# SwiGLU feed-forward on one core: the first weight slabs doubled, their queue changed, and both x tiles transposed before the first matmul

## The chip, the core and the metric

The kernel runs on one core of a Trainium2 chip. The metric is device time in microseconds (us) of one execution; the time before is the median of 3 runs. One more execution was taken by the profiler.

## The reference

```python
B, S, D, F = 1, 2048, 512, 1376     # x (B,S,D), w_gate and w_up (D,F), w_down (F,D), all bf16
def reference(x, w_gate, w_up, w_down):
    g = silu(x @ w_gate)
    u = x @ w_up
    return (g * u) @ w_down
```

## The kernel before

All instructions are written out by hand for five engines: SP (SyncE) and ACT (ScalarE) issue the loads, PE (TensorE) multiplies, ACT applies silu, DVE (VectorE) multiplies gate by up, and both ACT and DVE copy results out of PSUM. Semaphores order them.

**Tiles.** The hidden width F is cut into 10 full tiles of 128 and a rest of 96, the 2048 tokens into 4 chunks of 512, and the contraction over D into 4 steps (`dk`). The first stage makes, chunk by chunk, one gate group and one up group for each F tile: 4 matmuls of 128x128 weights with 512 tokens, into one of 8 PSUM banks in turn. ACT and DVE turn a pair of groups into a tile of `hT_sb`. The rest of 96 is packed into further groups: one for each chunk on PE (`X`, 4 matmuls of 512 tokens as well) and one for each two chunks (`Y`). The second stage multiplies by `w_down`, in strips of 32 rows, and stores 16 token tiles.

**x.** The matmuls need x with D on the partitions (`xT_sb`). For the first 256 tokens two tiles of 128 tokens are loaded as they are (`xn_sb`, `load_xn`, L113) and transposed on PE against an identity (`transposes`, L362), 4 transposes a tile, each into a bank of its own (banks 0 to 3 for tile 0, 4 to 7 for tile 1). DVE copies the even steps and ACT the odd ones into `xT_sb` (L300 and L288). `xt_ready[i, dk]` holds which engine makes the copy of tile i and step dk, and its place. All other tokens come through a transposing DMA (`load_x`, L93), tokens 256 to 383 and 384 to 511 in one each.

**Weights.** Gate and up weights come in slabs of F tiles (L104): tile 0, tile 1, tiles 2 and 3, tiles 4 to 6, the rest. One slab of one tile is 128 KB, read in runs of 256 B (128 columns of bf16); one of two tiles is 256 KB in runs of 512 B. ACT issues gate slab 0 and x tile 1 (`loads_on_scalar`, L119). SP issues x tile 0, up slab 0, the gate and up slabs of tile 1 and of tiles 2 and 3, the two transposing loads, and then all the rest (`loads_on_sync`, L123). A queue issues in order of the program and none of these loads waits for another.

**The order on PE.** PE starts with fillers on constants (`warm`, L354: 5 matmuls of 512 columns, 2 of 128). Then come the 4 transposes of x tile 0 (L371), 2 more fillers, gate tile 0 on the first 128 tokens, the transposes of x tile 1, up tile 0 on the first 128 tokens, and gate and up tile 0 on tokens 128 to 255, step by step. `first` is the list of the first 8 groups: gate and up of tiles 0 to 3 in turn. Groups 2 to 7 then run on the first 256 tokens in the order gate 1, up 1, gate 2, gate 3, up 2, up 3:

```python
for at in (2, 3, 4, 6, 5, 7):
    gu_matmuls(first[at], 0, HT)
```

After them groups 0 and 1 run on tokens 256 to 383 and 384 to 511, groups 2 to 7 on tokens 256 to 511, and from there on every group runs on 512 tokens at once. `gu_matmuls` (L347) waits for the slab that it needs, and `gu_step` (L339) in chunk 0 for the copies of the x tiles that its tokens lie in, each step for its own. A group counts as done (`s_P`) when its last token's last step is.

Of the kernel before, what the change touches and what calls it, by code (L numbers as in the profile page):

```python
# [11 lines left out]
N_GAP = 2  # L12


def bass_standalone__swiglu_ffn__prompt_kernel(nc, x, w_gate, w_up, w_down, out):
    _, S, D = x.shape
    F = w_gate.shape[1]
    P = 128
    KD = D // P
    NFF = F // P  # L20
    NFT = NFF + 1
# [7 lines left out]
    HT = SC // 2  # L29
    NXN = HT // P  # L30
    NB = 8
# [19 lines left out]
    with ExitStack() as es:  # L51
# [17 lines left out]
        banks = [bank_all[:, i, :] for i in range(NB)]  # L69
# [14 lines left out]
        def load_sem(name):  # L84
            loads[name] = sem(f"s_{name}")
            return loads[name]

        ones_w = nc.const_aps.tensor(1.0, [P, P], BF16)
        ones_m = nc.const_aps.tensor(1.0, [P, SC], BF16)
# [3 lines left out]
        def load_x(eng, name, t0, t1):  # L93
            eng.dma_start_transpose(
                xT_sb[:, :, t0:t1], xf[t0:t1, :]
            ).then_inc(load_sem(name), 16)

        def load_w(eng, name, src, base, f0, f1):
            eng.dma_start(
                w_sb[:, :, base + f0:base + f1],  # L100
                src[:, f0:f1].rearrange("(k p) f -> p k f", p=P),
            ).then_inc(load_sem(name), 16)

        slabs = [(0, 1), (1, 2), (2, 4), (4, 7), (7, NFT)]  # L104
        slab_of = {ft: a for a, b in slabs for ft in range(a, b)}

        def load_gate(eng, a, b):
            load_w(eng, f"wg{a}", w_gate, 0, a * P, min(b * P, F))

        def load_up(eng, a, b):  # L110
            load_w(eng, f"wu{a}", w_up, UPH, a * P, min(b * P, F - 32))

        def load_xn(eng, i):  # L113
            eng.dma_start(xn_sb[:, i, :], xf[i * P:(i + 1) * P, :]).then_inc(load_sem(f"xn{i}"), 16)
# [2 lines left out]
            return of[t * P:(t + 1) * P, :]  # L117

        def loads_on_scalar(act):  # L119
            load_gate(act, *slabs[0])  # L120
            load_xn(act, 1)

        def loads_on_sync(sp):  # L123
            load_xn(sp, 0)
            load_up(sp, *slabs[0])
            for a, b in slabs[1:3]:
                load_gate(sp, a, b)
                load_up(sp, a, b)
            load_x(sp, "x0b", HT, HT + P)
            load_x(sp, "x0c", HT + P, SC)  # L130
            for a, b in slabs[3:]:
                load_gate(sp, a, b)
                load_up(sp, a, b)
            load_w(sp, "wut", w_up, F - (F - 32), F - 32, F)
            for c in range(1, NSC):
                load_x(sp, f"x{c}", c * SC, (c + 1) * SC)
            sp.dma_start(
                wd_sb[:, 0:NFF, :], w_down[0:NFF * P, :].rearrange("(k p) d -> p k d", p=P)
            ).then_inc(load_sem("wd"), 16)
            load_sem("wdt")  # L140
            for y0 in (0, 64):
                sp.dma_start(wd_sb[y0:y0 + 64, T01, :], w_down[NFF * P:F - SR, :]).then_inc(loads["wdt"], 16)
            for x0 in range(0, P, SR):
                sp.dma_start(wd_sb[x0:x0 + SR, T2, :], w_down[F - SR:F, :]).then_inc(loads["wdt"], 16)
            sp.dma_start(wd_sb[0:F_LAST, TAIL, :], w_down[NFF * P:F, :]).then_inc(load_sem("wdl"), 16)
# [7 lines left out]
        def add_group(kind, **what):  # L153
            g = dict(kind=kind, at=len(groups), bank=banks[len(groups) % NB], readers=[], **what)
            groups.append(g)
            return g
# [8 lines left out]
        def tview(i, dk):  # L165
            return banks[KD * i + dk][:, 0:P // 2].bitcast(BF16)
# [46 lines left out]
        xt_ready = {}  # L213
# [19 lines left out]
        for at, t in enumerate(tiles):  # L233
# [3 lines left out]
            for c0, c1 in parts:  # L237
                g = add_group("O", t=t, c0=c0, c1=c1)
                eng = "A" if at % 2 == 1 and c0 == 0 else "D"
                op = add_op(  # L240
                    eng, g, kind="copy", out=o_sb[ob][:, c0:c1], src=g["bank"][:, 0:c1 - c0],
# [17 lines left out]
        def on_sync(sp):  # L259
            loads_on_sync(sp)  # L260
            store_tiles(sp, "S")
            for i in range(NOS):
                sp.wait_ge(s_out[i], 16 * n_store[i])
# [11 lines left out]
        def on_scalar(act):  # L275
            loads_on_scalar(act)
            act.activation(adummy[:, 0:4], zero_c, ACT.Silu)  # L277
            for op in act_ops:
                act.wait_ge(*ready(op))
                if op["kind"] == "silu":  # L280
                    if op["free"]:
                        act.wait_ge(s_D, op["free"])
                    fn = ACT.Silu
                else:
                    if op["stored"][1]:
                        act.wait_ge(*op["stored"])
                    fn = ACT.Copy
                act.activation(op["out"], op["src"], fn).then_inc(s_A, 1)  # L288
            store_tiles(act, "A")
# [13 lines left out]
        def on_tensor(pe):  # L303
            landed = set()

            def need(name, count=1):
                if name not in landed:
                    pe.wait_ge(loads[name], 16 * count)
                    landed.add(name)
# [3 lines left out]
            def after(eng, n):  # L313
                if n > read[eng]:
                    pe.wait_ge(s_A if eng == "A" else s_D, n)
                    read[eng] = n
# [6 lines left out]
            def whole(bank, dk, col, c, n0, n1):  # L323
                return pe.matmul(  # L324
                    bank[:, n0:n1], lhsT=w_sb[:, dk, col:col + P],
                    rhs=xT_sb[:, dk, c * SC + n0:c * SC + n1], start=(dk == 0), stop=(dk == KD - 1),
                )

            def gu_needs(g, n0, n1):
                c, ft = g["c"], g["ft"]  # L330
                if c > 0:
                    need(f"x{c}")
                if c == 0 and n1 > HT:
                    need("x0b")
                if c == 0 and n1 > HT + P:
                    need("x0c")
                need(("wg" if g["kind"] == "G" else "wu") + str(slab_of[ft]))

            def gu_step(g, dk, n0, n1):  # L339
                c = g["c"]  # L340
                col = (0 if g["kind"] == "G" else UPH) + g["ft"] * P
                if c == 0:
                    for i in range(n0 // P, min(n1 // P, NXN)):
                        after(*xt_ready[i, dk])
                ins = whole(g["bank"], dk, col, c, n0, n1)
                if n1 == SC and dk == KD - 1:
                    ins.then_inc(s_P, 1)  # L347

            def gu_matmuls(g, n0, n1):
                gu_needs(g, n0, n1)  # L350
                for dk in range(KD):
                    gu_step(g, dk, n0, n1)

            def warm(n, width):  # L354
                for i in range(n):
                    pe.matmul(banks[NB - 1][:, 0:width], lhsT=ones_w, rhs=ones_m[:, 0:width], start=True, stop=True)  # L356

            warm(N_WARM, SC)
            warm(N_FILL, P)
            pe.wait_ge(s_I, 1)  # L360

            def transposes(i):  # L362
                need(f"xn{i}")
                for dk in range(KD):
                    pe.matmul(  # L365
                        tview(i, dk), lhsT=xn_sb[:, i, dk * P:(dk + 1) * P], rhs=ident[:, :],
                        start=True, stop=True, is_transpose=True,
                    ).then_inc(s_X, 1)

            first = groups[0:NB]  # L370
            transposes(0)  # L371
            warm(N_GAP, P)
            gu_matmuls(first[0], 0, P)
            transposes(1)
            gu_matmuls(first[1], 0, P)
            for dk in range(KD):
                for g in first[0:2]:
                    gu_step(g, dk, P, HT)
            for at in (2, 3, 4, 6, 5, 7):
                gu_matmuls(first[at], 0, HT)  # L380
            for n0, n1 in ((HT, HT + P), (HT + P, SC)):
                for g in first[0:2]:
# [4 lines left out]
            for g in groups[NB:NO]:  # L387
# [11 lines left out]
                elif kind == "Y":  # L399
                    need(f"wu{slab_of[NFF]}")  # L400
                    for dk in range(KD):
                        for c in (2 * g["pi"], 2 * g["pi"] + 1):
# [3 lines left out]
                                rhs=xT_sb[:, dk, c * SC:(c + 1) * SC],  # L406
                                start=(dk == 0), stop=(dk == KD - 1),
# [61 lines left out]
            for g in groups[NO + TPC * (TPC - 1):]:  # L469
# [6 lines left out]
                for fk in (tailed if last else full[1:]):  # L476
                    if fk < NFF:
                        h, w = hT_sb[:, fk, t * P:(t + 1) * P], wd_sb[:, fk, c0:c1]
                    else:
# [3 lines left out]
                        stop=(fk == (NFF if last else NFF - 1)), skip_group_check=True,  # L483
# [4 lines left out]
        on_gpsimd(nc.gpsimd)  # L488
        on_scalar(nc.scalar)
        on_tensor(nc.tensor)  # L490
        on_vector(nc.vector)

# [27 lines left out]
```

## Time and profile before

| | us |
|---|---|
| time, median of 3 runs | 120.6 (120.32, 120.6, 120.76) |
| span of the profiled execution | 118.6 |
| TensorE (matmuls) busy in it | 115.9 |
| TensorE weight loads busy | 59.7 |
| DVE busy | 38.0 |
| ACT busy | 35.1 |

The profiled execution has no device time of its own beside its span, which runs from the first to the last instruction of the program; a run's time is longer by what lies around it. PE is TensorE's matmuls and PEld its weight loads, which overlap them. Matmuls are pipelined: their starts are recorded and their ends modelled, so that the busy time of PE holds gaps too short to see, and the spacing of starts says more than a length. A row of a timeline gives start, length, engine, line, operation, tiles, count, and in brackets the idle time ahead with what ended it; "ACTq" and "SPq" are DMA issues. The granted clock in the records stands at full speed over the whole span.

### The profile page before, as it was taken

What the parts mean: (1) busy time and instruction counts of PE and PEld (TensorE: products, weight loads), DVE (VectorE), ACT (ScalarE), POOL (GpSimd) and SP (SyncE); (2) the same over time, 40 slices, a digit from 0 to 9 for tenths busy, and PEclk for the clock granted to TensorE, in tenths of its full rate; (3) what the DMA queues carried; (4) which work ended last, traced back from release to release, by engine and by line L of the source; (5) the groups of instructions that cost most, each with busy time, mean ns of one, the idle gap of its engine ahead of it and who ended that gap; (6) DMA issues with size and microseconds to landing.
All of it is one profiled execution on the core that took longest, in us unless ns stands there. A gap on an engine that the chain in (4) does not pass through costs nothing.

```text
span 118.6 us, 2344 instructions
## 1 busy us (share of the span) xinstructions
PE 115.9 (98%) x1019; PEld 59.7 (50%) x1019; DVE 38.0 (32%) x60; ACT 35.1 (30%) x62; POOL 1.1 (1%) x7
## 2 busy tenths in 40 slices
PE   7999999999999999999999999999999999999993
PEld 2788444444444444444444444444444445885442
DVE  0206542444433444324444244360000044003321
ACT  3407334353244272343263432330000033003021
POOL 1000000000000000000000000010000000000000
PEclk9999999999999999999999999999999999999999
DMA  3999999991000000000000000000000017200612
GB/s 87 290 186 336 296 161 221 268 357 25 0 6 0 0 0 0 0 3 3 0 0 6 0 0 0 0 0 6 0 6 0 0 57 237 70 0 6 202 64 88
DMA packets 17642, 8.83 MB, mean 74 GB/s; under 512 B 10624, under 2 KB 17632, under 8 KB 17632
## 3 DMA queue, kind: packets, MB, share of 16 engines
q1 hardware_dynamic: 16816, 8.33, 27.3%
q10 hardware_dynamic: 816, 0.36, 1.1%
q8 instruction: 8, 0.13, 0.5%
q14 instruction: 2, 0.02, 0.0%
HBM read 4.75 MB, written 2.10 MB: 58 GB/s over the span
## 4 chain that ended last, share of the span: by engine, by line
PE 98%; DVE 0%; issue 0%
PE bank L324 62%; PE bank L442 25%; PE bank L481 7%; PE bank L356 2%; PE bank L404 2%; PE bank L365 1%; DVE o_sb L300 0%
## 5 line engine op out<-in xcount | busy, mean ns | idle before, releaser
L324 PE MATMUL bank<-xT_sb,w_sb 128*128 128x512 bf16 (+2 forms) x384 | 73.3, 352 | 0.1
L324 PEld LDWEIGHTS bank<-xT_sb,w_sb 128*128 128x128 bf16 x384 | 36.2, 98 | 36.8 <-DMA w_sb<-in_w_gate_dram 0.3
L296 DVE TENSOR_TENSOR hT_sb<-sg_sb,bank 128x512 bf16<-128x512 f32 x40 | 27.5, 688 | 40.2 <-PE bank L324 39.3
L288 ACT ACTIVATE sg_sb<-bank 128x512 f32<-128x512 f32 x40 | 23.9, 597 | 40.6 <-PE bank L324 40.5
L442 PE MATMUL bank<-wd_sb,hT_sb 32*128 32x512 bf16 x496 | 29.0, 374 | 0.0
L442 PEld LDWEIGHTS bank<-wd_sb,hT_sb 32*128 32x128 bf16 x496 | 15.2, 93 | 11.6 <-issue 0.4
L300 DVE CAST o_sb<-bank 128x512 bf16<-128x512 f32 (+1 forms) x10 | 5.7, 595 | 31.1 <-PE bank L442 25.9
L288 ACT ACTIVATE o_sb<-bank 128x512 bf16<-128x512 f32 (+1 forms) x8 | 4.3, 582 | 33.6 <-PE bank L442 27.9
L481 PE MATMUL bank<-wd_sb,hT_sb 128*128 128x512 bf16 (+2 forms) x56 | 8.1, 304 | 0.0
L481 PEld LDWEIGHTS bank<-wd_sb,hT_sb 128*128 128x128 bf16 x56 | 4.2, 98 | 4.2 <-issue 0.4
L442 PE MATMUL bank<-wd_sb,hy_sb 32*128 32x512 bf16 (+1 forms) x32 | 5.0, 371 | 0.0
L296 DVE TENSOR_TENSOR hx_sb<-sgx_sb,bank 32x512 bf16<-32x512 f32 x4 | 2.8, 692 | 3.5 <-ACT sgx_sb L288 3.5
L288 ACT ACTIVATE sgx_sb<-bank 32x512 f32<-32x512 f32 x4 | 2.4, 588 | 4.5 <-PE bank L324 4.5
L356 PE MATMUL bank<-const-bfloat16-1.0 128*128 128x512 bf16 (+1 forms) x9 | 2.8, 463 | 0.8 <-PEq L505 0.8
L442 PE MATMUL bank<-wd_sb,hx_sb 32*128 32x512 bf16 (+1 forms) x16 | 3.0, 371 | 0.0
L288 ACT ACTIVATE sgy_sb<-bank 64x512 f32<-64x512 f32 x4 | 2.4, 590 | 0.1
L356 PEld LDWEIGHTS bank<-const-bfloat16-1.0 128*128 128x128 bf16 x9 | 1.0, 128 | 2.2 <-issue 2.2
L300 DVE COPY xT_sb<-bank 128x128 bf16<-128x128 bf16 x4 | 0.8, 222 | 4.3 <-PE bank L365 4.3
L404 PE MATMUL bank<-xT_sb,w_sb 128*64 128x512 bf16 x16 | 1.9, 382 | 0.0
L442 PEld LDWEIGHTS bank<-wd_sb,hy_sb 32*128 32x128 bf16 x32 | 1.6, 93 | 0.6
L277 ACT ACT_TABLE_LOAD x1 | 1.3, 1283 | 1.9 <-issue 1.9
L404 PEld LDWEIGHTS bank<-xT_sb,w_sb 128*64 128x64 bf16 x16 | 0.8, 109 | 1.0 <-DVE hT_sb L296 0.4
(15 smaller groups left out, 6.6 us busy)
## 6 DMA issues: line engine op xcount, KB each, us to landing
out_dram<-o_sb SPq DMA_DIRECT2D x15, 128.0 KB, 1.8
wd_sb<-in_w_down_dram SPq DMA_DIRECT2D x1, 1280.0 KB, 7.3
w_sb<-in_w_gate_dram SPq DMA_DIRECT2D x1, 480.0 KB, 5.5
w_sb<-in_w_up_dram SPq DMA_DIRECT2D x1, 448.0 KB, 6.2
w_sb<-in_w_gate_dram SPq DMA_DIRECT2D x1, 384.0 KB, 4.3
w_sb<-in_w_up_dram SPq DMA_DIRECT2D x1, 384.0 KB, 4.7
w_sb<-in_w_up_dram SPq DMA_DIRECT2D x2, 128.0 KB, 3.2
w_sb<-in_w_gate_dram SPq DMA_DIRECT2D x1, 256.0 KB, 3.6
```

Source lines behind the costliest of these rows:

```text
L277: act.activation(adummy[:, 0:4], zero_c, ACT.Silu)
L288: act.activation(op["out"], op["src"], fn).then_inc(s_A, 1)
L296: ins = dve.tensor_tensor(op["out"], op["a"], op["b"], ALU.mult)
L300: ins = dve.tensor_copy(op["out"], op["src"])
L324: return pe.matmul(bank[:, n0:n1], lhsT=w_sb[:, dk, col:col + P], rhs=xT_sb[:, dk, c * SC + n0:c * SC + n1], start=(dk == 0), stop=(dk == ...
L356: pe.matmul(banks[NB - 1][:, 0:width], lhsT=ones_w, rhs=ones_m[:, 0:width], start=True, stop=True)
L365: pe.matmul(tview(i, dk), lhsT=xn_sb[:, i, dk * P:(dk + 1) * P], rhs=ident[:, :], start=True, stop=True, is_transpose=True,).then_inc(s_X, 1)
L404: ins = pe.matmul(g["bank"][y0:y1, :], lhsT=w_sb[:, dk, YC0:YC0 + 64], rhs=xT_sb[:, dk, c * SC:(c + 1) * SC], start=(dk == 0), stop=(dk == ...
L442: ins = pe.matmul(g["bank"][:, 0:c1 - c0], lhsT=h, rhs=wd_sb[r0:r0 + SR, w, c0:c1], start=(start and fk == fks[0]), stop=(stop and fk == f ...
L481: ins = pe.matmul(g["bank"][:, 0:c1 - c0], lhsT=h, rhs=w, start=(last and fk == 0), stop=(fk == (NFF if last else NFF - 1)), skip_group_ch ...
```

## The change

Three things are changed, all in the first 10 us.

- **Slabs and queues.** The slabs of tile 0 and of tile 1 become one of two tiles, for gate and for up. All weights are issued by SP: x tile 0, then gate and up of tiles 0 and 1, gate and up of tiles 2 and 3, and the rest as before, with one issue less ahead of it. ACT issues x tile 1 alone, as its first instruction.
- **Transposes.** Both x tiles are transposed in a row. The two fillers behind them wait for the first copy on DVE and write bank 0 instead of bank 7.
- **First matmuls.** Tiles 0 and 1 run on 256 tokens at once, both gates first: the order of the first eight groups is gate 0, gate 1, up 0, up 1, gate 2, gate 3, up 2, up 3.

```diff
-        slabs = [(0, 1), (1, 2), (2, 4), (4, 7), (7, NFT)]
+        slabs = [(0, 2), (2, 4), (4, 7), (7, NFT)]
...
         def loads_on_scalar(act):
-            load_gate(act, *slabs[0])
             load_xn(act, 1)
 
         def loads_on_sync(sp):
             load_xn(sp, 0)
-            load_up(sp, *slabs[0])
-            for a, b in slabs[1:3]:
+            for a, b in slabs[0:2]:
                 load_gate(sp, a, b)
                 load_up(sp, a, b)
             load_x(sp, "x0b", HT, HT + P)
             load_x(sp, "x0c", HT + P, SC)
-            for a, b in slabs[3:]:
+            for a, b in slabs[2:]:
...
-            def warm(n, width):
+            def warm(n, width, bank=banks[NB - 1]):
...
             first = groups[0:NB]
-            transposes(0)
-            warm(N_GAP, P)
-            gu_matmuls(first[0], 0, P)
-            transposes(1)
-            gu_matmuls(first[1], 0, P)
-            for dk in range(KD):
-                for g in first[0:2]:
-                    gu_step(g, dk, P, HT)
-            for at in (2, 3, 4, 6, 5, 7):
+            for i in range(NXN):
+                transposes(i)
+            after(*xt_ready[0, 0])
+            warm(N_GAP, P, banks[0])
+            for at in (0, 2, 1, 3, 4, 6, 5, 7):
                 gu_matmuls(first[at], 0, HT)
```

More of the change, by code (lines that the diff above doesn't have):

```diff
@@ L352, in gu_matmuls @@
                     gu_step(g, dk, n0, n1)
-            def warm(n, width):
+            def warm(n, width, bank=banks[NB - 1]):
                 for i in range(n):
-                    pe.matmul(banks[NB - 1][:, 0:width], lhsT=ones_w, rhs=ones_m[:, 0:width], start=True, stop=True)
+                    pe.matmul(bank[:, 0:width], lhsT=ones_w, rhs=ones_m[:, 0:width], start=True, stop=True)
             warm(N_WARM, SC)
```

## The prediction

> **What bounds the kernel now.** I read the head of the page first, then the whole chain of waits in order of time, then the list of who waited for whom, and last the timeline of the first 10 us, one engine at a time.
>
> ```profile
> span 118.6 us, 2344 instructions
> PE 115.9 (98%) x1019; PEld 59.7 (50%) x1019; DVE 38.0 (32%) x60; ACT 35.1 (30%) x62; POOL 1.1 (1%) x7
> ```
> ```profile
> 3.94 0.47 PE bank L324 x4
> 4.41 0.01 issue
> 4.42 0.40 PE bank L365 x4
> 4.81 1.65 PE bank L324 x20
> 6.46 0.00 issue
> 6.46 71.05 PE bank L324 x360
> ...
> 116.85 0.23 DVE o_sb L300
> ```
>
> TensorE is busy for 98% of the span and the chain (start, length, what) is TensorE nearly all the way. From 6.46 us on one piece of 71.05 us runs without any wait. So everything behind 6.46 us is a block that moves as a whole: the time changes by as much as the point from which the block runs is moved, and by nothing else that this diff does.
>
> How long the work itself takes comes from that piece. The first stage has four chunks of 21 groups, each with 4 x 512 columns: 172,032 columns. Before 6.46 us only tiles 0 and 1 have been done, gate and up, for 256 tokens: 4 groups x 4 x 256 = 4,096 columns. The other 167,936 took 71.05 us, 0.423 ns a column, so a 128x256 matmul costs 0.108 us, one group on 256 tokens (4 of them) 0.433 us, and the 4,096 columns 1.73 us. The first useful matmul starts at 3.94 us, so 6.46 - 3.94 = 2.52 us are used for 1.73 us of work: 0.79 us are lost. Put differently, an unbroken stream from 6.46 - 1.73 = **4.73 us** on would end at the same time as before. That is the mark the change must beat.
>
> Where the 0.79 us goes is in the timelines of PE, the weight loads, DVE and ACT (start, length, and in brackets the idle time ahead):
>
> ```profile
> 3.27 0.51 PE L365 MATMUL bank<-ident,xn_sb 128*128 128x128 bf16 x4
> 3.61 0.28 PE L356 MATMUL bank<-const-bfloat16-1.0 128*128 128x128 bf16 x2
> 3.94 0.47 PE L324 MATMUL bank<-xT_sb,w_sb 128*128 128x128 bf16 x4
> 4.42 0.40 PE L365 MATMUL bank<-ident,xn_sb 128*128 128x128 bf16 x4
> 4.65 0.94 PE L324 MATMUL bank<-xT_sb,w_sb 128*128 128x128 bf16 x12
> ```
> ```profile
> 3.57 0.41 DVE L300 COPY xT_sb<-bank 128x128 bf16<-128x128 bf16 x2 [3.57 <-PE bank L365]
> 4.68 0.35 DVE L300 COPY xT_sb<-bank 128x128 bf16<-128x128 bf16 x2 [0.70 <-PE bank L365]
> ```
> ```profile
> 3.68 0.45 ACT L288 ACTIVATE xT_sb<-bank 128x128 bf16<-128x128 bf16 x2 [0.31 <-PE bank L365]
> 4.74 0.45 ACT L288 ACTIVATE xT_sb<-bank 128x128 bf16<-128x128 bf16 x2 [0.61 <-PE bank L365]
> ```
> ```profile
> PEld bank L324 <- DMA w_sb<-in_w_gate_dram: 0.3, 1, 0.3
> ```
>
> The second tile's transposes stand inside the stretch (4.42 to 4.65, 0.23 us). Four 128-wide matmuls from 3.94 to 4.42 wait copy by copy and take 0.48 us for 0.22 us of work. And the third slab's gate weights are waited for at 6.46 us, 0.28 us by the weight loads.
>
> **The loads.** The SP queue's own timeline gives the issues, and the list of DMA issues in narrow windows gives each one's time to landing (last column, us):
>
> ```profile
> 0.81 0.40 SPq L114 DMA_DIRECT2D xn_sb<-in_x_dram  x1
> 1.27 0.42 SPq L99 DMA_DIRECT2D w_sb<-in_w_up_dram  x1
> ...
> 2.83 0.51 SPq L99 DMA_DIRECT2D w_sb<-in_w_gate_dram  x1
> 3.38 0.51 SPq L99 DMA_DIRECT2D w_sb<-in_w_up_dram  x1
> 3.93 2.60 SPq L94 DMA_TRANSPOSE xT_sb<-in_x_dram  x2
> 6.58 0.58 SPq L99 DMA_DIRECT2D w_sb<-in_w_gate_dram  x1
> 7.21 0.50 SPq L99 DMA_DIRECT2D w_sb<-in_w_up_dram  x1
> ```
> ```profile
> w_sb<-in_w_gate_dram SPq DMA_DIRECT2D x1, 384.0 KB, 4.3
> w_sb<-in_w_up_dram SPq DMA_DIRECT2D x1, 384.0 KB, 4.7
> ```
> ```profile
> w_sb<-in_w_gate_dram ACTq DMA_DIRECT2D x1, 128.0 KB, 2.8
> xn_sb<-in_x_dram SPq DMA_DIRECT2D x1, 128.0 KB, 2.3
> ```
> ```profile
> w_sb<-in_w_up_dram SPq DMA_DIRECT2D x1, 128.0 KB, 3.3
> xn_sb<-in_x_dram ACTq DMA_DIRECT2D x1, 128.0 KB, 3.1
> ```
> ```profile
> w_sb<-in_w_gate_dram SPq DMA_DIRECT2D x1, 256.0 KB, 3.6
> ```
> ```profile
> w_sb<-in_w_up_dram SPq DMA_DIRECT2D x1, 256.0 KB, 3.8
> ```
> ```profile
> xT_sb<-in_x_dram SPq DMA_TRANSPOSE x1, 4.0
> ```
> ```profile
> 4.00:4.50 0.50, 0.49 (x6) 0.31 (x7) 0.00 (x0) 0.12 (x1) 0.00 (x0) 1.00 1.16 257
> ...
> 5.50:6.00 0.50, 0.50 (x8) 0.44 (x6) 0.00 (x0) 0.00 (x0) 0.00 (x0) 1.00 1.13 331
> ```
>
> Landings: x tile 0 at 0.81 + 2.3 = 3.1, up slab 0 at 1.27 + 3.3 = 4.57, the gate slab of tiles 2 and 3 at 2.83 + 3.6 = 6.43 (the wait above), its up slab at 3.38 + 3.8 = 7.18. The last two columns of the windows are the DMA engines' share and rate: the engines are full, at 257 GB/s while slabs of one tile (256 B runs) are loaded and at 331 GB/s with slabs of two tiles (512 B runs). So the landings follow from bytes.
>
> **The change part by part.**
>
> *When the weights are there.* Ahead of the first gate slab now stand both x tiles (256 KB), and it has 256 KB itself. By 4.57 us the kernel before had landed just as many bytes: x 0, gate 0, x 1, up 0, 512 KB. Half of these would now go in 512 B runs: 262,144 B at 331 instead of 257 GB/s is 0.79 instead of 1.02 us, 0.23 us less. Gate slab 0 lands at 4.57 - 0.23 = 4.34 us. No load of before stands in the same place, so its bounds are wide: 1.27 + 2.3 = 3.57 by the x tile's row, 1.27 + 3.6 = 4.87 by the 256 KB row. I take 4.34, which counts bytes. Each further slab of 256 KB adds 0.79: up 0 at 5.13, gate 2 at 5.92, up 2 at 6.71.
>
> *When x is transposed.* Tile 0's transposes stay at 3.27 us (x tile 0 is still first on SP). Tile 1's follow at 3.61 if x tile 1 lands by then: issued at 0.81 instead of 1.31, it lands between 0.81 + 2.3 = 3.1 and 0.81 + 3.1 = 3.9 us. I take 3.5, since it now shares the engines with x tile 0 alone. The eight copies then bind: DVE and ACT do four each in a row. The third on DVE, needed by the first 256-wide matmul, starts at 3.57 + 0.41 = 3.98 and ends near 4.2. PE began 0.15 us after the end of its first copy before (3.57 + 0.22, then 3.94), so it begins at **4.35 us**. The fourth on ACT ends by 3.68 + 2 x 0.45 = 4.58; the fourth matmul needs it and would start at 4.35 + 3 x 0.108 = 4.67. Weights at 4.34 and copies give the same start. If x tile 1 lands at 3.9, tile 1's last copy ends 0.77 us behind (5.19 - 4.42, as before) at 4.7 and the stream starts about 0.1 us later.
>
> *The stream behind it.* Gate 0 and 1 take 2 x 0.433 = 0.87 us, so up 0 is needed at 5.22 (there at 5.13), gate 2 at 6.08 (5.92), up 2 at 6.95 (6.71): 0.1 to 0.2 us of slack each, and the wait of 0.28 us goes. Tokens 256 to 383 are needed at 4.35 + 3.47 = 7.82. Their transposing load landed at 3.93 + 4.0 = 7.93, 0.75 us behind the up slab ahead of it, so at 7.46 now; SP has one issue less ahead of it (0.55 us, 3.38 less 2.83). Unmoved it would cost 0.11 us. The next gate slab is needed at 4.35 + 32 x 0.217 = 11.28 and landed at 6.58 + 4.3 = 10.88 already before; its up slab is needed 0.87 us later, at 12.15, and landed at 7.21 + 4.7 = 11.91. Both now move up. Nothing is late next.
>
> *What costs nothing.* ACT loses one issue of some 0.5 us; its first copy waits for PE anyway (0.31 us idle ahead of 3.68). The two filler matmuls move behind the first DVE copy and write bank 0. Behind them on PE stands only gate 0, which waits for later copies; with 2 x 0.06 us they fit between 3.9 and 4.35. Without that cover they would cost 0.11 us. Sixteen fewer matmuls: a 128-wide one took 0.058 us (4.42 to 4.65 for four), half of 0.108, so nothing. The second halves keep their order, so the first silu and what follows move with the stream.
>
> *Sum.* The stream starts at 4.35 instead of the equivalent 4.73: 0.38 us less, a span of 118.2 us. The median of three runs stands at 120.6 us, 2.0 above the profiled span of 118.6; I keep that distance: **120.2 us**, 0.3% less, inside the 0.5% which a measurement of this kernel can tell from no change.
>
> **The rivals.**
>
> *The TensorE clock rises late (slower).* The fillers' weight loads show a slow start:
>
> ```profile
> 1.23 0.15 PEld L356 LDWEIGHTS bank<-const-bfloat16-1.0 128*128 128x128 bf16 x1 [0.28 <-issue]
> ...
> 2.93 0.15 PEld L356 LDWEIGHTS bank<-const-bfloat16-1.0 128*128 128x128 bf16 x1 [0.28 <-issue]
> ```
>
> Four steps of 512 columns take 1.70 us, 0.83 ns a column, twice the 0.423 of later. The rows of the transposes put the switch at about 3.3 to 3.9 us (four took 0.34 us from 3.27, then 0.23 us from 4.42). The change leaves PE idle for most of 3.85 to 4.35, and has no slack behind that to swallow slow matmuls, where before had its 0.79 us. Each us of slow stream costs 0.5 us: the 0.38 us is gone if the switch comes at 5.1, and it is slower by over 0.5% (0.6 us) from 4.35 + 2 x 0.98 = 6.3 on. A second stretch as long as the one from 0.84 to 3.6, counted from the start of the stream, would put it at 7.1: 1.4 us, 121.6 us. Against it: PE works from 0.84 to 3.85 without a pause, and the switch had come by then. [...]
>
> *The first slab lands by its size.* At 4.87, by the row of the 256 KB load, the stream starts at 4.9 and the time is 0.2 us longer: 120.8. For it: even a 128 KB slab took 3.3 us behind less. Against it: that row's load stood behind 768 KB, this one behind 256.
>
> *Nothing moves.* The slack of 0.1 to 0.2 us is used up, and PE waits for up 0 or gate 2 instead: a gate 2 slab at 6.43 as before gives 6.43 - 1.73 = 4.70, the old time, 120.6.
>
> *More than counted.* Gate 0 and the copies come 0.25 us earlier: 0.63 us, 120.0 or a little below. The copies of before make that hard to reach.
>
> **How the numbers follow.** Forecast 0.60 (119.95 to 120.45, the runs of before differ by 0.44); late first slab 0.12; nothing moves 0.08; more than counted 0.10; late clock 0.10. The range 119.8 to 120.85 holds all but most of the late clock and a part of the fastest case. Faster by over 0.5% (below 120.0) is the fastest case and a corner of the forecast: 0.15. Slower by over 0.5% (above 121.2) is the upper part of the late clock: 0.06. The rest, 0.79, is within 0.5%.
>
> **What the changed profile would show.** Eight transposes in a row from about 3.3; the first 256-wide matmul at 4.35; no wait for weights until the tail; loads at 1.27 landing near 4.3; the long piece of PE starting at 4.35 instead of 6.46. Wrong would be: a first matmul behind 4.7, a wait on an up slab near 5.2, or 256-wide matmuls 0.21 us apart.

## The result and the profile after

The changed kernel takes **120.88 us** (median of 20 runs), the kernel before 120.33 us (20 runs): ratio 1.0037, 95% interval 1.0019 to 1.0055. It is slower by 0.55 us by the medians, by 0.45 us by the ratio, where 0.4 us less was forecast, and lies just outside the range. Ratios here and below leave out executions more than 1.5% above the fastest of their kernel (here 122.52 and 696.66 us), while medians are of all runs. A caution on its size: in the last experiment a copy of the kernel before, measured as if it were another kernel, came out at 1.0032 (1.0011 to 1.0054) against the kernel before. So such an interval holds the scatter within one set of runs, not all that differs from set to set. That the forecast gain is not there is clear; that it has become a loss rests on this median lying above those of all eight sets of the kernel before (120.1 to 120.6).

The profiled execution after took 120.79 us, its span is 119.5 us. The page's head, then the chain of waits:

```profile
span 119.5 us, 2327 instructions
```
```profile
0.81 2.72 DMA xn_sb<-in_x_dram
3.53 0.14 issue
3.67 1.01 PE bank L363 x8
4.68 0.21 PE bank L354 x2
4.89 73.54 PE bank L322 x376
...
117.77 0.23 DVE o_sb L298
```

The stream is unbroken as the change wants it, but the last piece starts 0.92 us later than before (117.77 instead of 116.85). The timelines of PE, DVE and ACT say how it starts:

```profile
3.67 1.01 PE L363 MATMUL bank<-ident,xn_sb 128*128 128x128 bf16 x8 [0.32 <-DMA xn_sb<-in_x_dram]
4.47 0.42 PE L354 MATMUL bank<-const-bfloat16-1.0 128*128 128x128 bf16 x2
4.77 4.43 PE L322 MATMUL bank<-xT_sb,w_sb 128*128 128x256 bf16 x31
```
```profile
3.97 0.86 DVE L298 COPY xT_sb<-bank 128x128 bf16<-128x128 bf16 x4 [3.97 <-PE bank L363]
```
```profile
4.08 0.92 ACT L286 ACTIVATE xT_sb<-bank 128x128 bf16<-128x128 bf16 x4 [1.33 <-PE bank L363]
```

Eight transposes start at 3.67 instead of 3.27 us, and the first matmul at 4.77 instead of the forecast 4.35. How fast the stream then runs is seen by counting weight loads, one for each matmul, in two stretches of 1.86 us (columns: stretch, length, busy time and count, granted clock, DMA share and rate):

```profile
4.74:6.60 1.86, 1.32 (x10) 1.00 1.20 308
6.60:8.46 1.86, 1.65 (x17) 1.00 1.05 203
```

Ten against seventeen: nine matmuls of 256 columns take 0.21 us each, and only from about 6.6 us on 0.109 us. The granted clock is 1.00 in both rows, but that column counts time without a clock record as full speed, and this trace kept no record; here the halving is seen only in the spacing. Where a trace kept one, the record of full speed starts at the switch: at 3.55 us in the profile of before (so, other than stated ahead of the prediction, it does not cover the whole span) and at 9.82 us in e1 below. Nine matmuls at twice the time are 0.9 us more. In this execution the first rival happened: the start is 0.4 us later than forecast, which puts it 0.04 us behind the mark of 4.73, and the slow stretch has cost the other 0.9 us.

The weights, from the list of DMA issues in narrow windows (last column: us to landing):

```profile
w_sb<-in_w_gate_dram SPq DMA_DIRECT2D x1, 256.0 KB, 3.1
```
```profile
w_sb<-in_w_up_dram SPq DMA_DIRECT2D x1, 256.0 KB, 3.6
```
```profile
w_sb<-in_w_gate_dram SPq DMA_DIRECT2D x1, 256.0 KB, 4.1
```

Issued at 1.26, 1.73 and 2.27 us, they land at 4.34, 5.32 and 6.39. The first is what the forecast said (4.34). The next two are late (5.13 and 5.92 were forecast); here nothing waits for them, since TensorE comes to them late itself. At full speed from 4.77 on it would have needed them at 5.64 and 6.50 (4 groups on 256 tokens take 1.73 us), so in this execution they were in time either way.

### The profile page after: what moved, and what is told of

It is laid out like the page before. It is cut to its first block, busy times and chain, and to the rows that moved or that the text cites. A ratio compares the mean times of both kernels' runs of the same rounds, so it can differ in the third digit from the quotient of the medians.

```text
span 119.5 us, 2327 instructions
## 1 busy us (share of the span) xinstructions
PE 116.6 (98%) x1011; PEld 60.3 (50%) x1011; DVE 38.1 (32%) x60; ACT 35.1 (29%) x62; POOL 1.1 (1%) x7
## 4 chain that ended last, share of the span: by engine, by line
PE 95%; DMA 2%; issue 0%; DVE 0%
PE bank L322 62%; PE bank L436 25%; PE bank L475 7%; DMA xn_sb<-in_x_dram 2%; PE bank L398 2%; PE bank L363 1%; DVE o_sb L298 0%; PE bank L354 0%
```

## The experiments

Two theories stood at first. L: the loss is the late landing of x tile 0. C: the loss is the slow stretch, which the unbroken stream cannot swallow. A third came out of the first runs, W: the 256 KB up slab of tiles 0 and 1 lands late. Medians are of each kernel's own runs, ratios are to the kernel before on the same chip.

### Loads alone, order alone

The changed kernel with TensorE's old order, and the kernel before with the new one:

```diff
-            for i in range(NXN):
-                transposes(i)
...
-            for at in (0, 2, 1, 3, 4, 6, 5, 7):
+            transposes(0)
+            warm(N_GAP, P)
+            gu_matmuls(first[0], 0, P)
+            transposes(1)
...
+            for at in (2, 3, 4, 6, 5, 7):
```

> The changed kernel's loads with TensorE's old order. Theory L (x tile 0 lands late): tile 0 still lands near 3.5 instead of 3.1 us, the first gate matmul moves to about 4.3, up slab 0 is waited for until 5.3, and the unbroken stream is some 0.4 us later than before: about 120.7 us where before stands at 120.33. Theory C (the clock rises late and the unbroken stream has no waits in which to swallow slow matmuls): the old order keeps its waits, so no more than 0.1 us over before: 120.3 to 120.45.

> The old loads with TensorE's new order. Theory L: x tile 0 lands at 3.1 again, x tile 1 at 4.4, its last copy at 5.2, the stream is worth a start at 4.9 instead of 4.73: about 120.5 us. Theory C: the stream is as exposed to a late clock as in the changed kernel, another 0.2 to 0.3 us: 120.7 to 120.8, and 256-wide matmuls 0.21 us apart wherever the switch comes behind 4.9.

Measured: loads alone 122.71 us, ratio 1.0173 (1.0146 to 1.02), far off what either theory said; order alone 120.64, ratio 1.0009 (0.9981 to 1.0037), with four of its 12 runs at 121.98 to 122.70 (its profile is of one of these, 122.12). The chain of the first names the wait:

```profile
1.73 4.03 DMA w_sb<-in_w_up_dram
5.76 0.05 issue
5.81 74.52 PE bank L322 x380
```

The up slab landed at 5.76 us, and with the old order TensorE sat idle for it from 5.2 to 5.8. Its matmuls then stayed at half speed (0.21 us for 256 columns) until 9.8 us, three microseconds longer than in the changed kernel. This is the first sign of W, and of a link between idle time ahead and the end of the slow stretch. The order with the old loads is not told from no change: its median lies between the forecasts of L (120.5) and C (120.7 to 120.8).

### x tile 0 first, and the idle time ahead of the stream

Both x tiles on SP (e3), more fillers ahead of the transposes (e4), both in the changed kernel:

```diff
         def loads_on_scalar(act):
-            load_xn(act, 1)
...
             load_xn(sp, 0)
+            load_xn(sp, 1)
```
```diff
-N_FILL = 2
+N_FILL = 7
```

e7 makes e3's edit in the kernel before, where ACT keeps gate slab 0. e8 makes it in the changed kernel and gives gate slab 0 to ACT; e12 adds fillers to that:

```diff
         def loads_on_scalar(act):
-            load_xn(act, 1)
+            load_gate(act, *slabs[0])
...
             load_xn(sp, 0)
-            for a, b in slabs[0:2]:
+            load_xn(sp, 1)
+            load_up(sp, *slabs[0])
+            for a, b in slabs[1:2]:
```
```diff
                 transposes(i)
+                if i == 0:
+                    warm(7, P)
```

> The changed kernel with x tile 1 behind x tile 0 on SP, nothing on ACT. Theory L: x tile 0 lands at 3.1 again and tile 1 by 3.4, all moves up by 0.4 us: about 120.45 us. Theory C: an earlier start only puts more matmuls under the slow clock, so at most half of the 0.4 us comes back: about 120.7.

> The changed kernel with 5 more 128-column fillers, so that TensorE does not idle between 3.14 and 3.67 us. Theory C in the form that this idle time holds the clock back: the switch comes near 3.6 in most executions, as in the profile of before, and the time is 120.3 to 120.5. If the switch falls at a random point whatever TensorE does there, or under theory L alone: 120.9, no change.

> The kernel before with x tile 1 on SP right behind x tile 0; gate slab 0 stays alone on ACT. Tile 1 should land near 3.6 instead of 4.4 and its transposes follow the first gate matmuls without a wait. Theory C: in executions with an early clock the gate slab of tiles 2 and 3 (6.4 us) still binds, so nothing; with a late one 0.2 us of idle time goes: 120.2 to 120.35 where before stands at 120.45. Theory L: the same loads in front, no change, 120.45.

> The changed kernel with gate slab 0 (256 KB) alone on ACT, and x tile 1 on SP behind x tile 0: x tile 0 should land at 3.1 again, tile 1 near 3.6, the gate slab at 4.3, and the stream start at 4.35 as forecast. Theory L: all of the 0.4 us comes back, 120.0 to 120.1. Theory C: the start comes back, but half of it is lost again wherever the clock rises later than 4.4: 120.3 to 120.6.

> The changed kernel with gate slab 0 on ACT and x tile 1 second on SP, and now 7 fillers of 128 columns between the two tiles' transposes, where TensorE idled for 0.7 us and 4 of 12 runs took 121.8 us and more. Theory C: the idle time makes the clock come late, so no run above 121.5, and the median near 120.4. If the late runs have another cause: a third of the runs above 121.5 again.

| run | x 0 lands | x 1 | gate 0 | up 0 | median | ratio (95%) |
|---|---|---|---|---|---|---|
| e3 | 2.96 | 3.46 | 5.01 | 6.34 | 120.73 | 1.0027 (1.0001 to 1.0053) |
| e4 | 3.60 | 3.79 | 4.46 | 6.25 | 120.74 | 1.0025 (1.0004 to 1.0046) |
| e7 | 3.17 | 3.91 | 3.61 | 5.36 | 120.67 | 1.0035 (1.0020 to 1.0049) |
| e8 | 3.18 | 4.37 | 4.00 | 5.39 | 120.81 | 1.0037 (1.0009 to 1.0065) |
| e12 | 2.97 | 4.25 | 3.90 | 5.72 | 120.47 | 1.0015 (0.9996 to 1.0034) |

L gets its mechanism and not its price. With x tile 1 issued on ACT at the same moment, x tile 0 lands at 3.5 to 3.6 (e4, e1 and the changed kernel); with a weight slab on ACT, or nothing, at 3.0 to 3.3. But putting that right moves the wait to the next load: in e3 x comes early and gate 0 at 5.0, in e8 x tile 1 at 4.4. None of them gave 0.4 us back. The fillers of e4 did not move the time either (in its profile the fast stretch starts at 6.4, against 6.6 in the changed kernel), so the form of C that blames the pause at 3.14 us falls.

e7 was slower than both forecasts (120.2 to 120.45). In its profile the clock is up from 3.95 us, and TensorE then sits idle from 4.6 to 5.4 us for up slab 0, as its chain says:

```profile
1.73 3.63 DMA w_sb<-in_w_up_dram
5.36 0.05 issue
5.41 7.27 PE bank L324 x76
```

So in this execution a late slab costs time in the old order too, and without any hold.

e8 and e12 differ only in seven fillers. PE's timeline of e8, then of e12:

```profile
3.32 0.58 PE L365 MATMUL bank<-ident,xn_sb 128*128 128x128 bf16 x4
4.42 0.43 PE L365 MATMUL bank<-ident,xn_sb 128*128 128x128 bf16 x4 [0.51 <-DMA xn_sb<-in_x_dram]
```
```profile
3.14 0.63 PE L365 MATMUL bank<-ident,xn_sb 128*128 128x128 bf16 x4
3.57 0.80 PE L356 MATMUL bank<-const-bfloat16-1.0 128*128 128x128 bf16 x7
4.30 0.40 PE L365 MATMUL bank<-ident,xn_sb 128*128 128x128 bf16 x4
```

Four of 12 runs of e8 took 121.8 us or more, none of e12 (at most 120.95); e2, with a like pause ahead of the second tile's transposes, had four of 12 as well. A split of four to none comes about once in 20 times by chance, so this is a hint, and what C says: idle time ahead of the stream makes slow stretches longer.

What sets the end of the slow stretch was not shown: the record of full speed starts at 3.55 us in the profile of before, at 8.75 in e2 and at 9.82 in e1, and of the pairs that differ in fillers alone, the changed kernel and e4 switched at 6.6 and 6.4, and e8 and e12 give the hint above. It may be in part a matter of chance.

e12 is the best of these versions, and not told from the kernel before.

### The clock taken out

Both kernels with all loads held back for 6 us by copies on ACT, while TensorE runs fillers; in the second form 12 fillers of 512 columns behind the hold instead of 9:

```diff
+            sp.wait_ge(s_H, 1)
             loads_on_sync(sp)
...
+            for i in range(N_HOLD):
+                ins = act.activation(hold_sb[:, i * SC:(i + 1) * SC], ones_m, ACT.Copy)
+            ins.then_inc(s_H, 1)
+            act.wait_ge(s_H, 1)
             loads_on_scalar(act)
...
             warm(N_FILL, P)
+            warm(9, SC)
+            pe.wait_ge(s_H, 1)
+            warm(9, SC)             # 12 in the second form
```

> The kernel before with all loads held back by nine 512-column copies on ACT, some 6 us, while TensorE runs 9 more fillers of 512 columns before and 9 after the hold: the clock is up before x arrives. Only its difference to the changed kernel with the same hold counts. Theory C: every 128x512 filler behind the hold takes 0.216 us, and the time scatters less than the 1.0 us of before. If the clock has no part in it, it scatters as before.

> The changed kernel with the same hold. Theory C (the loss is slow matmuls under a late clock): the 0.45 to 0.55 us against before goes, and it is within 0.1 us of the held kernel before, since x tile 0 landing 0.4 us late eats what the unbroken stream gains. Rival (the loss is late loads and order alone): it stays 0.4 to 0.5 us slower than the held kernel before.

> The held kernel before, with 12 instead of 9 fillers behind the hold, so that TensorE is busy until x tile 0 lands. Theory C (idle TensorE time ahead of the stream lets the clock fall or come late): as the held kernel before, 126.1 to 126.4, all runs within 0.5 us.

> The held changed kernel with 12 fillers behind the hold. Its first form had two groups of runs, near 126.2 and near 126.9. Theory C: the upper group is the clock once more, and goes: all runs within 0.3 us of the held kernel before with the same fillers. Rival (the upper group is weights that land late, which a filled pause can't change): two groups again, half the runs or more near 126.9.

Measured: held 126.17 (before; 4 runs from 125.99 to 126.33; 1.0487, 1.0461 to 1.0514) and 126.87 (changed; 6 runs, two at 126.01 and 126.32, four near 126.9; 1.0528, 1.0499 to 1.0558). Held and filled: 126.42 (1.0495, 1.0461 to 1.0529) and 126.89 (1.0538, 1.0505 to 1.0571). The clock was up in both: the clock records of three of the four traces start at 6.35 to 6.58 us, ahead of x (9.35 and later), and the matmuls on x run at full speed in the fourth (e10 has 18 weight loads in the 1.86 us from 12.5 us on, where the profile after had 10 in its slow stretch and 17 behind it). The changed kernel is still slower, by 0.5 to 0.7 us by the medians, as much as without the hold (the intervals of each pair of ratios overlap a little). The upper group of its runs did not go with the fillers. Theory C as the cause of this difference falls; its rival, late loads and order, has it. PE's timeline of the held and filled changed kernel shows what is left:

```profile
9.91 0.61 PE L374 MATMUL bank<-ident,xn_sb 128*128 128x128 bf16 x8
10.45 0.29 PE L362 MATMUL bank<-const-bfloat16-1.0 128*128 128x128 bf16 x2
10.80 1.10 PE L330 MATMUL bank<-xT_sb,w_sb 128*128 128x256 bf16 x8
12.54 5.65 PE L330 MATMUL bank<-xT_sb,w_sb 128*128 128x256 bf16 x58 [0.64 <-DMA w_sb<-in_w_up_dram]
```

Gate 0 and 1 run (8 matmuls), and then TensorE waits for up slab 0. Its issue, and that of the gate slab ahead of it (7.93 and 7.46 us):

```profile
w_sb<-in_w_up_dram SPq DMA_DIRECT2D x1, 256.0 KB, 4.6
```
```profile
w_sb<-in_w_gate_dram SPq DMA_DIRECT2D x1, 256.0 KB, 3.2
```

It lands 1.8 us behind gate slab 0 for 256 KB, where 0.79 us was forecast.

The kernel before, held and filled, does not go free either. Its profile has two waits of the weight loads (total, times, longest), for the gate slabs of tile 1 and of tiles 2 and 3; the second row is the wait of the changed kernel:

```profile
PEld bank L332 <- DMA w_sb<-in_w_gate_dram: 0.8, 2, 0.4
```
```profile
PEld bank L330 <- DMA w_sb<-in_w_up_dram: 0.9, 1, 0.9
```

These two executions are only 0.12 us apart (126.72, the slowest of e9, and 126.84). So late weights cost both kernels, and the changed one seems to pay more of the time.

### The late slab taken out

The same held and filled kernels, with up slab 0 alone loaded ahead of the hold (e13), with all first slabs ahead of it (e14, changed; e15, before), and with slabs of one tile in the same order (e11):

```diff
+            load_up(sp, *slabs[0])
             sp.wait_ge(s_H, 1)
             loads_on_sync(sp)
...
             for a, b in slabs[0:2]:
                 load_gate(sp, a, b)
-                load_up(sp, a, b)
+                if a:
+                    load_up(sp, a, b)
```
```diff
+            for a, b in slabs[0:2]:
+                load_gate(sp, a, b)
+                load_up(sp, a, b)
             sp.wait_ge(s_H, 1)
             loads_on_sync(sp)
```
```diff
-        slabs = [(0, 2), (2, 4), (4, 7), (7, NFT)]
+        slabs = [(0, 1), (1, 2), (2, 4), (4, 7), (7, NFT)]
...
+            load_gate(sp, 0, 1)
+            load_gate(sp, 1, 2)
+            load_up(sp, 0, 1)
+            load_up(sp, 1, 2)
```

The first of these is e13, the second e14 (the loads are gone from their old place; e15 does the same to the six slabs of the kernel before), the third e11.

> The held and filled changed kernel with only up slab 0 loaded ahead of the hold. Theory W (the 256 KB up slab lands late and stops the unbroken stream, 0.9 us of wait in the profile of the held and filled kernel): the wait goes, and with it 0.5 to 0.8 us: 126.1 to 126.4. If the loss is in the start of the stream (x tile 0 late, copies): no more than 0.1 us comes back, 126.8.

> The same with all four first weight slabs ahead of the hold: only x is late, so the copies alone bind the start. Theory W: as the run with up slab 0 alone or 0.1 us less, 126.0 to 126.3. Start theory: 126.7.

> The held and filled kernel before with its first six weight slabs ahead of the hold. The broken stream is left with its waits for x tile 1 and its copies. The forecast had the unbroken stream 0.38 us ahead where weights are not late: then 0.3 to 0.4 us above the changed kernel of this group. If the broken stream uses the waits as well as the unbroken one: equal within 0.1 us.

> The held and filled changed kernel with slabs of one tile again for tiles 0 and 1 (gate 0, gate 1, up 0, up 1 on SP). By the forecast's count of bytes narrow runs cost 0.23 us for each 256 KB, so gate 0 lands sooner (half the bytes), up 0 and up 1 not later than 0.5 us behind: within 0.1 us of the run above if copies bind the start, up to 0.4 us slower if the width of the runs counts as forecast.

| run | median | lowest to highest | ratio (95%) |
|---|---|---|---|
| e10, changed, own loads | 126.89 | 126.58 to 127.13 | 1.0538 (1.0505 to 1.0571) |
| e13, up 0 early | 125.98 | 125.75 to 126.68 | 1.0501 (1.0474 to 1.0529) |
| e14, all first weights early | 125.76 | 125.75 to 125.79 | 1.0468 (1.0450 to 1.0487) |
| e15, before, all first weights early | 125.81 | 125.80 to 125.81 | 1.0472 (1.0454 to 1.0490) |
| e9, before, own loads | 126.42 | 126.08 to 126.72 | 1.0495 (1.0461 to 1.0529) |
| e11, slabs of one tile | 126.96 | 126.87 to 127.13 | 1.0542 (1.0512 to 1.0573) |

One DMA taken out of the race gives 0.9 us by the medians and 0.4 us by the ratios, whose intervals overlap (the two sets ran apart, on chips where the kernel before stood at 120.30 and 120.13). It takes 256 KB out of the queue, not a delay alone: the slab that is now second, gate of tiles 2 and 3, lands 1.5 us behind gate slab 0 (12.01), but it is needed only at 12.4. The wait is gone from PE's timeline of e13:

```profile
10.57 7.66 PE L332 MATMUL bank<-xT_sb,w_sb 128*128 128x256 bf16 x73
```

With all first weights there, the two orders are equal: 125.76 and 125.81, and the scatter of the runs shrinks to 0.04 us. The chains of e14 and e15 show it to the hundredth; the stream behind the copies starts at 10.59 in one and 10.93 in the other, and both pieces end at 17.83:

```profile
9.96 0.63 DVE xT_sb L306 x4
10.59 0.00 issue
10.59 7.24 PE bank L330 x72
```
```profile
10.29 0.42 PE bank L330 x4
10.70 0.22 PE bank L374 x4
10.93 6.90 PE bank L330 x76
```

The unbroken stream starts late because it waits for all copies, and the broken one fills that time with work. So 0.05 us is what the order is worth, once weights are there and x tile 1 lands soon behind x tile 0: in e15 it comes at 9.80, where it came at 10.62 in e9, because gate slab 0 no longer stands ahead of it on ACT. Against their own loads (e9 and e10) the kernel before gains 0.6 us and the changed one 1.1 by the medians. That difference of 0.5 us is the whole loss with the clock up.

Slabs of one tile (e11) make it no better: there gate 1 landed 1.75 us behind gate 0, for 128 KB in runs of 256 B. So a slab can be late without wide runs. What the width is worth e11 does not tell, since its stream waits for the gate slab of tiles 2 and 3 in the end (13.65), which is issued 1.1 us later than in e10.

### The clock surely low

The held pair of the first form without fillers beside the hold:

```diff
             warm(N_FILL, P)
-            warm(9, SC)
             pe.wait_ge(s_H, 1)
-            warm(9, SC)
```

> The held kernel before without the fillers beside the hold: TensorE idles for 6 us ahead of x, so the stream starts at the slow clock (matmuls of 256 columns 0.21 us apart). Only its difference to the changed kernel of the same form counts.

> The changed kernel with the hold and no fillers beside it. Theory C (the new order has nothing behind it that swallows slow matmuls): slower than the held cold kernel before by more than the 0.45 to 0.5 us between the two with the clock up, 0.6 to 1.0. Theory W (the late up slab is the loss): at the slow clock the slab is there before it is needed, so less than 0.5 us: 0.2 to 0.4, half of the difference in the start of the stream.

Measured: 127.2 (126.62 to 128.09), ratio 1.0581 (1.0536 to 1.0626), and 127.76 (126.92 to 128.04), ratio 1.0602 (1.0567 to 1.0636). The medians are 0.56 us apart, the intervals overlap, the runs of each scatter by more than 1 us. Both kernels lose 0.8 to 1.0 us without the fillers beside the hold (against 126.17 to 126.42 and 126.87 to 126.89), and this pair does not tell whether one loses more. W expected that the slow clock gives the slab time to land. In the profile of e17 it did not: up slab 0 came at 12.67, 2.2 us behind gate slab 0, and the weight loads waited 0.4 us for it in the middle of the slow stretch (9 of them in the 1.86 us from 11.2 us on, against 18 at full speed in e10).

### The kernel before once more

> The kernel before once more, for a second profile with a time of its own. All other profiles lie 1.3 us under their execution's time, so the first profile of before (span 118.6) belongs to an execution of 119.9 us, the fastest there are, and not to the median. If so: time and span again 1.3 us apart, and a span of 118.6 to 119.6, longer the later the spacing of matmuls falls from 0.107 to 0.056 us for 128 columns. If the 2.0 us that the prediction put between span and time were right: a span near 118.4 at a time of 120.4.

Measured: 120.58 us (8 runs), ratio 1.0032 to the kernel before, for the same code. Its profiled execution took 119.88 us; the page's head of that profile:

```profile
span 118.6 us, 2344 instructions
```

Time and span are 1.3 us apart, as in the changed kernel (120.79 and 119.5), and not 2.0. The first profile of before, with the same span, was therefore an execution of about 119.9 us, near the shortest there are (119.81).

## Why the prediction was wrong

- **"Each further slab of 256 KB adds 0.79" failed.** With the clock up, this is the step that turned the gain into a loss: TensorE waits 0.9 us for up slab 0 in the profile of e10, and 0.9 us by the medians come back with that slab early (e13). Gate slab 0 landed as forecast (4.34 forecast; 4.34, 4.40, 4.46 in three profiles with these loads). Up slab 0 was to land at 5.13 and came at 5.32, 5.76 and 6.25 in the same three, gate slab 2 at 6.39, 6.69 and 7.00 instead of 5.92. The rate of 331 GB/s was a mean over all DMA engines, and the kernel waits for the last of 16 increments of a slab's semaphore. For up slab 0 these came from 4.86 to 5.32 in the profile after, and from 4.97 to 6.25 in that of e4: seven of them by 5.01, the last 1.2 us behind. Why some were late stays open: single packets of 512 B took up to 1.1 us in that profile, against 0.03 us in the median. The 0.1 to 0.2 us of slack was an average's slack.
- **"Tile 0's transposes stay at 3.27 us" failed.** x tile 0 landed at 3.53 because x tile 1 now starts beside it (2.96 to 3.18 in e3, e7, e8 and e12, where it does not): 37 and 106 GB/s flowed in the half microseconds from 1.5 and 2.0, instead of 61 and 183. The first matmul came at 4.77 instead of 4.35. In the profiled execution this step alone eats the forecast gain, since 4.77 lies behind the mark of 4.73.
- **The 0.38 us for the unbroken stream** fell with it. With weights out of the way and TensorE at the transposes equally early in both (9.71 and 9.66), the order is worth 0.05 us. In e15 the old order has neither the wait for a slab nor the late x tile 1 that the forecast counted against it, and it loses nothing to the new one.
- **The late clock** was priced rightly (0.5 us for each us) and given too little weight: the profiled execution has it, for 1.9 us of the stream. The reason against it was that TensorE works to 3.85 without a pause and the switch had come by then; x tile 0 late made a pause behind 3.15, but e4 has no such pause and switched at 6.4 all the same, so the pause is not shown to be the cause. And the switch at 3.55 was that of one of the shortest executions. With the clock up the changed kernel loses as much, so the late clock is not needed to tell the two apart. In the profile after, with a slow stretch, nothing waits for the late slab; with the clock up it is paid. How the executions of the kernel as it stands divide between the two was not measured, so for that kernel the shares of the slow stretch and of the late slab in the 0.45 us stay open.
- **The 2.0 us between span and median** was wrong: 1.3 us lie around the span, and the rest was that the profile of before showed one of its kernel's shortest executions. A change's gain on that execution's waits is not the gain on the median.
- **What held:** the wait for the gate slab of tiles 2 and 3 is gone, nothing came late behind it (the next gate slab landed at 9.6, needed past 12), and the block behind moved as a whole. One count was off without effect: there are eight matmuls fewer (1011 instead of 1019), not sixteen.

## What to carry to other kernels

A transfer that is due within 0.2 us of its use, where the landings of one slab scatter by 0.9 us (5.32 to 6.25 here), should be taken as late: plan by the last landing seen over several executions, not by bytes over a mean rate, and put the slack where the scatter is. A stream without gaps is worth no more than one with gaps if it has to start later by their sum: in e14 and e15 both had done the same work by 17.83 us. And ask of which execution a profile is: where the runs scatter by 1 us, a gap of 0.3 us in one profile is no budget.

## What was not expected of the hardware

- With the first weights loaded early and the clock up, runs of a 126 us kernel agree within 0.04 us; with their own loads they scatter by 0.34 to 0.94 us (e5, e6, e9, e10), and as they stand by 1 us. So almost all scatter of this kernel arises from its first loads and the slow stretch.
- With x tile 1 issued in the same moment on ACT and weights behind it, x tile 0 took 2.67 to 2.79 us to land (the changed kernel, e1, e4, e6, e10, e11, e17); with a weight slab on ACT, or nothing, 2.15 to 2.51. With weights loaded ahead of both (e13 to e15) it took 2.37 to 2.57 beside x tile 1.
- The slow stretch of TensorE does not show in the granted-clock column, which takes time without a record for full speed (1.00). It ended anywhere from 3.5 to 9.8 us in the profiles without a hold, and where a clock record was kept, it starts there (3.52 and 3.55 in the kernel before, 8.75 in e2, 9.82 in e1).
